# The first product of a gated network in two 64-row tiles of TensorE's array, with copies of its moving operand in the other half

## The chip, the core and the metric

The kernel runs on one core of a Trainium2 chip. Time is device time in microseconds (us) of one execution; the median of three runs before the change is 2152.42 us (2152.29 to 2153.91). PE is TensorE's matmul stream, PEld its weight loads, DVE VectorE, ACT ScalarE, POOL GpSimd and SP SyncE, which issues the transfers.

## What is computed

Four batches of 12480 rows with 128 channels go through attention over 49 agents and then through a two-layer network of width 2048:

```python
def _attn_ref(q, k, v, agents):
    a2k = sm(agents, k)          # softmax(scale * agents @ k.T), 49 x 12480
    agent_v = a2k @ v            # 49 x 128
    q2a = sm(q, agents)          # 12480 x 49
    return q2a @ agent_v
def _moe_ref(x, w_in, w_out):    # 128 -> 2048 -> 128
    h = x @ w_in
    g = h - np.tanh(h)
    return g @ w_out
```

## The kernel before, in words

The kernel folds the attention's last product into the network's first layer. Per batch it computes `agent_v`, multiplies it with `w_in` (`project`), and so has a matrix of 49 x 2048. A row of the output then needs only its 49 softmax weights p: h is p times that matrix. Both are in f32, and a single-pass product keeps fewer bits, so each operand is split in a high and a low part: `awh` and `awl` for the matrix, and for p the two parts stacked. The matrix is held twice, in partitions 0 to 48 and 49 to 97, and the transposed p (`pT`) has its high part in the first 49 partitions and its low part in the next 49. One matmul of 98 rows then gives awh x (p high + p low).

The rows are cut into 100 blocks of up to 500 rows, 25 per batch, and the 2048 hidden columns into 16 chunks of 128; two chunks are a **pair**, so there are 8 pairs per block and 800 in all. For each pair:

- `m1` (L531 to L536): four matmuls of 98 rows and 500 columns on TensorE, for each chunk one with `awh` (L534) and one with `awl` (L535). Their result `h` fills two PSUM banks, one per chunk; there are three such buffers.
- ACT makes `y` = tanh (L544) and `z` = y squared (L546); DVE makes `g` = h times z (L549), a form of h - tanh(h) for small h.
- POOL rounds `g` to its high part `gh` (L578), and DVE takes the low part `gl` (L583).
- `m2` (L596 to L598): six matmuls into the block's accumulator, for each chunk `gh` with the low part of `w_out`, `gh` with its high part, and `gl` with the high part. Every second block's last pair, and the first block, use one f32 matmul per chunk in place of three (L594).

Between the pairs small pieces of other work are started at fixed positions of a pair of blocks: the softmax of the next two blocks (`q_softmax`, L490 to L513), their transposes (`q_transpose`, L521 and the copy to `pT` at L526) at position 13 for the even block and position 2 for the odd one, and the attention over k and v of the next batch (`phase1`, L278, L329 and L339 on TensorE). L278 and L339 use 64 columns of the array, two products at a time in different halves. The order in which an engine gets its instructions is made by a scheduler that plays through the program with estimated times; fixed orders are given only for the first block and, in a few places, for DVE, ACT and POOL. All transfers go through SP's queue in order.

A check at the end (`general`) repeats all with a slower formula where h is too large; it isn't taken with these inputs.

Of the kernel before, what the change touches and what calls it, by code (L numbers as in the profile page):

```python
# [12 lines left out]
F32 = mybir.dt.float32  # L13
F32R = mybir.dt.float32r
# [3 lines left out]
ET = mybir.EngineType  # L18
AF = mybir.ActivationFunctionType
ALU = mybir.AluOpType  # L20
# [3 lines left out]
B, N, C = 4, 12480, 128  # L24
A = 49
A2 = 2 * A
EARLY = 11
HALF = 64
FF = 2048
NCH = FF // 128  # L30
TT = 126
TG = 120
GT = 8
# [4 lines left out]
BT = GT // 2  # L38
BLK = 500
# [57 lines left out]
class Build:  # L97
# [19 lines left out]
    def constants(self):  # L117
        nc = self.nc
        c = self.const
        self.agz = c.tile([128, B, HALF], F32, tag="ag", name="ag")  # L120
        self.ag = self.agz[:, :, :A]
        nc.sync.dma_start(self.ag, self.agT.rearrange("b c a -> c b a"))
        nc.gpsimd.memset(self.agz[:, :, A:], 0.0)
        self.ident = c.tile([128, 128], F32, tag="ident", name="ident")
        make_identity(nc, self.ident)
        self.identr = c.tile([128, 128], F32R, tag="identr", name="identr")
        nc.vector.tensor_copy(self.identr, self.ident)
        self.sel = c.tile([128, A], F32, tag="sel", name="sel")
        for r in (slice(0, HALF), slice(HALF, 128)):
            nc.vector.tensor_copy(self.sel[r], self.ident[r, r.start : r.start + A])  # L130
        self.ones = c.tile([128, 128], F32, tag="ones", name="ones")
        nc.vector.memset(self.ones, 1.0)
        self.mx = c.tile([128, NP * B], F32, tag="mx", name="mx")
        nc.vector.memset(self.mx, 0.0)
        self.w_in = c.tile([128, FF], F32, tag="w_in", name="w_in")
        self.wo_h = c.tile([128, NCH, C], F32R, tag="wo_h", name="wo_h")
        self.wo_l = c.tile([128, NCH, C], F32R, tag="wo_l", name="wo_l")
        self.wo_f = c.tile([128, 2, C], F32, tag="wo_f", name="wo_f")
        self.vb = [c.tile([128, GT, C + 2], F32, tag=f"v{i}", name=f"v{i}") for i in range(VB)]
        self.avs = c.tile([128, B, A2], F32, tag="avs", name="avs")  # L140
        self.aw = {}

    def decode(self, raw, dst, size, rem, ta, tb):
# [51 lines left out]
    def phase1(self, b):  # L195
        nc = self.nc
# [35 lines left out]
        def scores(g):  # L232
# [42 lines left out]
            for c in range(n // 2):  # L275
                for r in range(2):
                    to = ps[HALF * r : HALF * (r + 1), c * 128 : (c + 1) * 128]
                    nc.tensor.matmul(to, self.agz[:, b, :], kt[:, n // 2 * r + c, :], start=True, stop=True)  # L278
# [118 lines left out]
        def sums():  # L397
            yield
            yield
            if b == 0:  # L400
                an, n = st["acc"], HALF + A
                nc.vector.tensor_copy(an[:n, :C], st["ps"][:n, :C])
                pt = self.misc()
                nc.tensor.matmul(pt[:, :A], an[:n, :C], self.sel[:n], start=True, stop=True)
                sm = self.small.tile([128, A], F32, tag="mb", name="mb")
                nc.vector.tensor_scalar(sm, st["pr"], EPS, None, ALU.add)
                nc.vector.reciprocal(sm, sm)
                yield
                two = [128, 2, A]
                nc.vector.tensor_tensor(  # L410
                    self.avs[:, b, :].rearrange("p (two a) -> p two a", a=A),
                    pt[:, None, :A].broadcast_to(two),
                    sm[:, None, :].broadcast_to(two),
                    ALU.mult,
                )
                return
            acc = st["acc"]
            pt = self.misc()
            nc.tensor.matmul(pt[:, :A], acc[:, :C], self.sel, start=True, stop=True)
            rows_of = acc[:, C : C + 1].broadcast_to([128, 128])  # L420
            nc.tensor.matmul(pt[:, A:A2], rows_of, self.sel, start=True, stop=True)
            yield
            sm = self.small.tile([128, A], F32, tag="sm", name="sm")
            nc.vector.tensor_scalar(sm, pt[:, A:A2], EPS, None, ALU.add)
            nc.vector.reciprocal(sm, sm)
            two = [128, 2, A]
            nc.vector.tensor_tensor(
                self.avs[:, b, :].rearrange("p (two a) -> p two a", a=A),
                pt[:, None, :A].broadcast_to(two),
                sm[:, None, :].broadcast_to(two),  # L430
                ALU.mult,
            )

        if b == 0:
            self.mb_at = lambda: st["mb_at"]
# [6 lines left out]
    def project(self, b, bound):  # L442
        nc = self.nc

        def part(c, lo, hi):
            yield
            yield
            if c == 0:
                self.aw[b] = tuple(
                    self.keep.tile([128, FF], F32R, tag=t, name=t, bufs=2) for t in ("awh", "awl")  # L450
                )
            awh, awl = self.aw[b]
            sl = slice(lo, hi)
            if b == 0 and bound and c < 2:
                ps = self.ph.tile([128, 2, 512], F32, tag="h", name="h")[:, 0, :]
            else:
                ps = self.misc()
            ps = ps[:A2, : hi - lo]
            nc.tensor.matmul(ps, self.avs[:, b, :], self.w_in[:, sl], start=True, stop=True)
            yield  # L460
            h = awh[:A2, sl]
            nc.scalar.copy(h, ps)
            nc.vector.tensor_tensor(awl[:A2, sl], ps, h.bitcast(F32), ALU.subtract)
            if bound and b:
                self.bound(b, c, sl)

        cuts = PCUT if b == 0 and bound else (0, 512, 1024, 1536, 2048)
        return [part(c, cuts[c], cuts[c + 1]) for c in range(len(cuts) - 1)]
# [15 lines left out]
    def q_softmax(self, halves, qt, res, TT=TT):  # L484
        nc = self.nc
        ps = self.misc()
        for t in range(GT):
            b, at, w = halves[t // BT]
            at += min(t % BT * TT, w - TT)
            nc.tensor.matmul(ps[:TT, t * A : (t + 1) * A], qt[:, at : at + TT], self.ag[:, b, :], start=True, stop=True)  # L490
            if t % BT == BT - 1:
                yield
        pv = ps[:TT, : GT * A].rearrange("p (t a) -> p t a", a=A)
        m = self.small.tile([128, GT], F32, tag="qm", name="qm")
        e = self.small.tile([128, GT, A], F32, tag="qe", name="qe")
        ev = e[:TT]
        s = self.small.tile([128, GT], F32, tag="qs", name="qs")
        nc.vector.tensor_reduce(m[:TT], pv, axis=AX.X, op=ALU.max)
        nc.scalar.copy(ev, pv)  # L499
        yield  # L500
        nc.gpsimd.tensor_tensor(ev, ev, m[:TT, :, None].broadcast_to([TT, GT, A]), ALU.subtract)  # L501
        yield
        nc.scalar.activation(ev, ev, AF.Exp, scale=SCALE)
        yield
        nc.vector.tensor_reduce(s[:TT], ev, axis=AX.X, op=ALU.add)
        nc.vector.tensor_scalar(s[:TT], s[:TT], EPS, None, ALU.add)
        nc.vector.reciprocal(s[:TT], s[:TT])
        nc.vector.tensor_tensor(ev, ev, s[:TT, :, None].broadcast_to([TT, GT, A]), ALU.mult)
        yield
        pp = self.small.tile([128, GT, A2], F32R, tag="pp", name="pp")  # L510
        nc.scalar.copy(pp[:TT, :, :A], ev)  # L511
        yield
        nc.gpsimd.tensor_tensor(pp[:TT, :, A:], ev, pp[:TT, :, :A].bitcast(F32), ALU.subtract)  # L513
        res.append(pp)

    def q_transpose(self, pp, half, res, w, TT=TT):
        nc = self.nc
        ps = self.misc()
        for t in range(BT):
            at = min(t * TT, w - TT)  # L520
            nc.tensor.transpose(  # L521
                ps[:A2, at : at + TT].bitcast(F32R), pp[:TT, half * BT + t, :], self.identr[:TT, :TT]
            )
        yield
        pT = self.keep.tile([128, BLK], F32R, tag="pT", name="pT", bufs=3)
        nc.scalar.copy(pT[:A2, :w], ps[:A2, :w])  # L526
        res.append(pT)

    def m1(self, aw, pT, i, w):
        nc = self.nc  # L530
        h = self.ph.tile([128, 2, 512], F32, tag="h", name="h")  # L531
        for c in range(2):
            sl = slice((2 * i + c) * 128, (2 * i + c + 1) * 128)
            nc.tensor.matmul(h[:, c, :w], aw[0][:A2, sl], pT[:A2, :w], start=True, stop=False)  # L534
            nc.tensor.matmul(h[:, c, :w], aw[1][:A2, sl], pT[:A2, :w], start=False, stop=True)  # L535
        return h[:, :, :w]  # L536

    def pair(self, t):
# [364 lines left out]
```

## Time and profile before

| | |
|---|---|
| median of three runs | 2152.42 us (2152.29 to 2153.91) |
| span of the profiled execution | 2150.6 us |
| the profiled execution's own time beside the span | not recorded; the runs' median is 1.8 us longer |
| busy: PE, PEld | 2126.8, 1713.6 us |
| busy: DVE, ACT, POOL | 1998.3, 1828.1, 1313.8 us |
| granted clock of TensorE, mean | 0.998 |
| transfers | 108.69 MB, 15.1% of 16 engines' span |

A row of a group gives line, engine, operation, output <- inputs, the shape and count, then busy time and mean duration in ns, then the idle time of the engine just before, and what ended it. In rows of the timeline the first number is the start in us from the span's start and the second the time to the end of the row's last instruction; a row with x16 holds sixteen in a row. Matmuls are pipelined, so a duration is longer than the distance to the next start. An f32 matmul leaves two records. `98*128` is the number of rows and columns of the array that are in use.

### The profile page before, as it was taken

The page shows a single profiled execution, that of the slowest core. Times are in us where ns is not written, and L with a number is a line of the kernel's source. Part 1 is how long each engine was busy: PE and PEld are TensorE (multiplying, and loading weights), DVE is VectorE, ACT ScalarE, POOL GpSimd, SP SyncE. Part 2 cuts the span into 40 slices and gives each one's busy share as a digit, 9 for nine tenths or more (in the row PEclk, how much of TensorE's full clock was granted, in tenths as well). Part 3 has the DMA queues.
Part 4 walks back from the last instruction along what each step waited for, and adds up shares of the span by engine and source line. Part 5 has one row for each costly group of instructions (what it writes and reads, how often), then busy time and mean ns, then how long its engine had stood idle before and what let it go on. Part 6 is the DMA issues. An engine that isn't in the chain of part 4 may idle for free.

```text
span 2150.6 us, 30293 instructions
## 1 busy us (share of the span) xinstructions
PE 2126.8 (99%) x10859; PEld 1713.6 (80%) x10859; DVE 1998.3 (93%) x2031; ACT 1828.1 (85%) x2136; POOL 1313.8 (61%) x858
## 2 busy tenths in 40 slices
PE   8999999999999999999999999999999999999998
PEld 7587878877877887888787778878878888888886
DVE  7999998889999998889999999988999999999998
ACT  3888888888888888888898888888889889899896
POOL 0365566556665565556675557655566767777666
PEclk9999999999999999999999999999999999999999
DMA  9321112110111111111002110111000000000000
GB/s 350 96 67 60 52 34 73 51 49 29 39 49 59 60 50 49 59 61 49 20 20 68 59 42 28 51 59 41 28 31 20 29 30 20 29 29 20 29 10 21
DMA packets 65325, 108.69 MB, mean 51 GB/s; under 512 B 3984, under 2 KB 44176, under 8 KB 65168
## 3 DMA queue, kind: packets, MB, share of 16 engines
q1 hardware_dynamic: 65168, 106.68, 15.1%
q8 instruction: 89, 1.46, 0.3%
q14 instruction: 68, 0.56, 0.1%
HBM read 81.10 MB, written 25.56 MB: 50 GB/s over the span
## 4 chain that ended last, share of the span: by engine, by line
PE 95%; DVE 2%; POOL 1%; issue 1%; ACT 0%; DMA 0%; POOLq 0%; SPq 0%; DVEq 0%
PE h L534 17%; PE h L535 16%; PE misc L598 16%; PE misc L596 15%; PE misc L597 15%; PE misc L594 4%; PE misc L490 4%; PE misc L339 2%; PE misc L278 2%; PE misc L521 1%; PE h L249 1%; POOL gh L578 1%; DVE g L549 1%; PE misc L329 1%; DVE gl L583 1%
## 5 line engine op out<-in xcount | busy, mean ns | idle before, releaser
L578 POOL TENSOR_SCALAR gh<-g 128x1000 fp32r<-128x1000 f32 (+1 forms) x743 | 1172.7, 1579 | 702.9 <-DVE g L549 357.9
L583 DVE TENSOR_TENSOR gl<-g,gh 128x1000 fp32r<-128x1000 f32 (+1 forms) x743 | 952.8, 1284 | 99.9 <-PE misc L598 58.9
L549 DVE TENSOR_TENSOR g<-h,z 128x1000 f32<-128x1000 f32 (+1 forms) x800 | 946.1, 1187 | 24.6 <-ACT z L546 20.6
L544 ACT ACTIVATE y<-h 128x1000 f32<-128x1000 f32 (+1 forms) x800 | 799.0, 1002 | 191.6 <-PE h L535 187.6
L546 ACT ACTIVATE z<-y 128x1000 f32<-128x1000 f32 (+1 forms) x800 | 828.8, 1040 | 21.2 <-DVE g L549 4.2
L534 PE MATMUL h<-pT,awh 98*128 98x500 f32 (+1 forms) x1600 | 662.1, 414 | 0.1
L535 PE MATMUL h<-pT,awl 98*128 98x500 f32 (+1 forms) x1600 | 623.1, 389 | 0.0
L598 PE MATMUL misc<-gl,wo_h 128*128 128x500 f32 (+1 forms) x1486 | 589.5, 397 | 3.7 <-DVE gl L583 3.7
L596 PE MATMUL misc<-gh,wo_l 128*128 128x500 f32 (+1 forms) x1486 | 579.0, 390 | 2.8 <-POOL gh L578 2.8
L597 PE MATMUL misc<-gh,wo_h 128*128 128x500 f32 (+1 forms) x1486 | 578.1, 389 | 0.0
L534 PEld LDWEIGHTS h<-pT,awh 98*128 98x128 f32 x1600 | 301.2, 188 | 77.4 <-issue 14.0
L535 PEld LDWEIGHTS h<-pT,awl 98*128 98x128 f32 x1600 | 303.0, 189 | 67.7 <-issue 14.7
L598 PEld LDWEIGHTS misc<-gl,wo_h 128*128 128x128 f32 x1486 | 279.1, 188 | 70.0 <-DVE gl L583 10.5
L596 PEld LDWEIGHTS misc<-gh,wo_l 128*128 128x128 f32 x1486 | 280.8, 189 | 62.6 <-POOL gh L578 7.8
L597 PEld LDWEIGHTS misc<-gh,wo_h 128*128 128x128 f32 x1486 | 279.7, 188 | 54.5
L501 POOL TENSOR_TENSOR qe<-qe,qm 126x392 f32<-126x392 f32 x50 | 69.7, 1395 | 65.3 <-ACT qe L499 65.3
L513 POOL TENSOR_TENSOR pp<-qe,pp 126x392 fp32r<-126x392 f32 x50 | 67.8, 1357 | 58.4 <-ACT pp L511 56.6
L490 PEld LDWEIGHTS misc<-ag,qt 128*126 128x126 f32 x800 | 95.9, 190 | 3.9
L490 PE MATMUL misc<-ag,qt 128*126 128x49 f32 x800 | 93.4, 269 | 0.0
L594 PE MATMUL misc<-g,wo_f 128*128 128x500 f32 (+1 forms) x196 | 89.9, 581 | 0.0
L754 ACT ACTIVATE o<-misc 128x500 f32<-128x500 f32 (+1 forms) x100 | 58.2, 582 | 21.7 <-PE misc L598 11.7
L526 ACT CAST pT<-misc 98x500 fp32r<-98x500 f32 (+1 forms) x100 | 56.7, 568 | 7.4 <-PE misc L521 6.5
(111 smaller groups left out, 840.5 us busy)
## 6 DMA issues: line engine op xcount, KB each, us to landing
kt<-kT SPq DMA_DIRECT2D x48, 512.0 KB, 3.7
qt<-qT SPq DMA_DIRECT2D x46, 500.0 KB, 3.4
outT<-o SPq DMA_DIRECT2D x46, 500.0 KB, 2.6
v<-v SPq DMA_DIRECT2D x36, 512.0 KB, 4.1
vt<-v SPq DMA_DIRECT2D x12, 512.0 KB, 7.1
raw<-w_in SPq DMA_DIRECT2D x4, 512.0 KB, 9.0
v<-w_out SPq DMA_DIRECT2D x4, 512.0 KB, 8.9
qt<-qT SPq DMA_DIRECT2D x4, 490.0 KB, 3.4
```

Of the source, the lines that this page charges most:

```text
L490: nc.tensor.matmul(ps[:TT, t * A : (t + 1) * A], qt[:, at : at + TT], self.ag[:, b, :], start=True, stop=True)
L534: nc.tensor.matmul(h[:, c, :w], aw[0][:A2, sl], pT[:A2, :w], start=True, stop=False)
L535: nc.tensor.matmul(h[:, c, :w], aw[1][:A2, sl], pT[:A2, :w], start=False, stop=True)
L544: nc.scalar.activation(self.pair(y), h, AF.Tanh, scale=TSC)
L546: nc.scalar.activation(z, y, AF.Square)
L549: nc.vector.tensor_tensor(self.pair(g), h, self.pair(z), ALU.mult)
L578: self.nc.gpsimd.tensor_scalar(gh, g, 1.0, 0.0, ALU.mult, ALU.add)
L583: self.nc.vector.tensor_tensor(gl, g, gh.bitcast(F32), ALU.subtract)
L594: nc.tensor.matmul(acc[:, :w], wf[:, c * C : (c + 1) * C], gh[:, x], start=first, stop=last)
L596: nc.tensor.matmul(acc[:, :w], self.wo_l[:, f, :], gh[:, x], start=first, stop=False)
L597: nc.tensor.matmul(acc[:, :w], self.wo_h[:, f, :], gh[:, x], start=False, stop=False)
L598: nc.tensor.matmul(acc[:, :w], self.wo_h[:, f, :], gl[:, x], start=False, stop=last)
```

## The change

The two parts of p are no longer multiplied in one matmul of 98 rows. The high part now stands in partitions 0 to 48 and the low part in 64 to 112 (`HALF` is 64, `PW` is 113), the matrices `awh` and `awl` are held in both places (`av2`), and two transfers per block copy the parts of p to the other half into a second tile, `pb`. In `m1` the first chunk of a pair uses only partitions 0 to 48, the second only 64 to 112: each is a product of 49 rows in its own 64-row half of the array. A chunk needs three terms: awh x p low, awl x p high and awh x p high. The term awl x p low is left out. The matmuls are written alternately for the two chunks, and their order among themselves is fixed. `pT` has two buffers instead of three, and `pb` has two. The tiles for the softmax's result (`pp`) are two fixed ones, cleared once.

```diff
@@ q_softmax
-        pp = self.small.tile([128, GT, A2], F32R, tag="pp", name="pp")
+        pp = self.ppb[self.npp % 2]
+        self.npp += 1
         nc.scalar.copy(pp[:TT, :, :A], ev)
         yield
-        nc.gpsimd.tensor_tensor(pp[:TT, :, A:], ev, pp[:TT, :, :A].bitcast(F32), ALU.subtract)
+        nc.gpsimd.tensor_tensor(pp[:TT, :, HALF:PW], ev, pp[:TT, :, :A].bitcast(F32), ALU.subtract)
@@ project
             if c == 0:
+                for at in (0, HALF):
+                    nc.vector.tensor_copy(self.av2[:, at : at + A], self.avs[:, b, :])
...
-            nc.tensor.matmul(ps, self.avs[:, b, :], self.w_in[:, sl], start=True, stop=True)
+            nc.tensor.matmul(ps, self.av2, self.w_in[:, sl], start=True, stop=True)
@@ q_transpose
-        pT = self.keep.tile([128, BLK], F32R, tag="pT", name="pT", bufs=3)
-        nc.scalar.copy(pT[:A2, :w], ps[:A2, :w])
-        res.append(pT)
+        pT = self.keep.tile([128, BLK], F32R, tag="pT", name="pT", bufs=2)
+        nc.scalar.copy(pT[:PW, :w], ps[:PW, :w])
+        pb = self.keep.tile([128, BLK], F32R, tag="pb", name="pb", bufs=2)
+        nc.sync.dma_start(pb[HALF:PW, :w].bitcast(F32), pT[:A, :w].bitcast(F32))
+        nc.sync.dma_start(pb[:A, :w].bitcast(F32), pT[HALF:PW, :w].bitcast(F32))
+        res.append((pT, pb))
@@ m1
-        for c in range(2):
-            sl = slice((2 * i + c) * 128, (2 * i + c + 1) * 128)
-            nc.tensor.matmul(h[:, c, :w], aw[0][:A2, sl], pT[:A2, :w], start=True, stop=False)
-            nc.tensor.matmul(h[:, c, :w], aw[1][:A2, sl], pT[:A2, :w], start=False, stop=True)
+        high, low = pT, pT[::-1]
+        first = self.count()
+        for n, (weights, p) in enumerate(((aw[0], low), (aw[1], high), (aw[0], high))):
+            for c, r in enumerate((slice(0, A), slice(HALF, PW))):
+                sl = slice((2 * i + c) * 128, (2 * i + c + 1) * 128)
+                nc.tensor.matmul(h[:, c, :w], weights[r, sl], p[c][r, :w], start=n == 0, stop=n == 2)
+        self.issue_order(ET.PE, first)
```

How the scheduler places the new instructions, the following pieces of the order show. First TensorE before the change, in the middle of the program: the first product of a pair (L534, L535) and then the second product of an earlier one.

```order
L534 MATMUL h<-pT,awh 128x500
L535 MATMUL h<-pT,awl 128x500
L534 MATMUL h<-pT,awh 128x500
L535 MATMUL h<-pT,awl 128x500
L598 MATMUL misc<-gl,wo_h 128x500
L596 MATMUL misc<-gh,wo_l 128x500
L597 MATMUL misc<-gh,wo_h 128x500
L598 MATMUL misc<-gl,wo_h 128x500
L596 MATMUL misc<-gh,wo_l 128x500
L597 MATMUL misc<-gh,wo_h 128x500
```

Ten matmuls all use the whole height of the array. The same place of TensorE's order after the change (the first product is L539 there, the second L601 to L603):

```order
L539 MATMUL h<-pb,awh 128x500
L539 MATMUL h<-pT,awh 128x500
L539 MATMUL h<-pT,awl 128x500
L539 MATMUL h<-pb,awl 128x500
L539 MATMUL h<-pT,awh 128x500
L539 MATMUL h<-pb,awh 128x500
L603 MATMUL misc<-gl,wo_h 128x500
L601 MATMUL misc<-gh,wo_l 128x500
L602 MATMUL misc<-gh,wo_h 128x500
L603 MATMUL misc<-gl,wo_h 128x500
L601 MATMUL misc<-gh,wo_l 128x500
L602 MATMUL misc<-gh,wo_h 128x500
```

Six matmuls of half the array's height now stand between those of the full height; the first reads `pb`, the tile that the transfers fill. The third place is the start of an even block on TensorE after the change (numbers tell the tiles apart: h_6818 and h_6843 are two pairs' results, pb_6776 and pT_6774 the new block's p).

```order
L601 MATMUL misc_6673<-gh_6785,wo_l_89 128x500
L602 MATMUL misc_6673<-gh_6785,wo_h_88 128x500
L539 MATMUL h_6818<-pb_6776,awh_5298 128x500
L539 MATMUL h_6818<-pT_6774,awh_5298 128x500
L539 MATMUL h_6818<-pT_6774,awl_5299 128x500
L539 MATMUL h_6818<-pb_6776,awl_5299 128x500
L539 MATMUL h_6818<-pT_6774,awh_5298 128x500
L539 MATMUL h_6818<-pb_6776,awh_5298 128x500
L539 MATMUL h_6843<-pb_6776,awh_5298 128x500
L539 MATMUL h_6843<-pT_6774,awh_5298 128x500
L539 MATMUL h_6843<-pT_6774,awl_5299 128x500
L539 MATMUL h_6843<-pb_6776,awl_5299 128x500
```

The block's first pairs moved to behind the second products of the block before, 18 of which stand between this block's transposes (L520) and the first row that reads pb_6776; three pairs' first products, 18 matmuls, then follow each other.

More of the change, by code (lines that the diff above doesn't have):

```diff
@@ L28 @@
 HALF = 64
+PW = HALF + A
 FF = 2048
@@ L130, in constants @@
             nc.vector.tensor_copy(self.sel[r], self.ident[r, r.start : r.start + A])
-        self.ones = c.tile([128, 128], F32, tag="ones", name="ones")
-        nc.vector.memset(self.ones, 1.0)
+        self.one = c.tile([128, 1], F32, tag="ones", name="ones")
+        nc.vector.memset(self.one, 1.0)
+        self.ones = self.one.broadcast_to([128, 128])
         self.mx = c.tile([128, NP * B], F32, tag="mx", name="mx")
@@ L139, in constants @@
         self.vb = [c.tile([128, GT, C + 2], F32, tag=f"v{i}", name=f"v{i}") for i in range(VB)]
-        self.avs = c.tile([128, B, A2], F32, tag="avs", name="avs")
+        self.avs = c.tile([128, B, A], F32, tag="avs", name="avs")
+        self.av2 = c.tile([128, PW], F32, tag="av2", name="av2")
+        nc.gpsimd.memset(self.av2, 0.0)
+        self.ppb = [c.tile([128, GT, PW], F32R, tag=f"pp{i}", name=f"pp{i}") for i in range(2)]
+        for t in self.ppb:
+            nc.gpsimd.memset(t.bitcast(F32), 0.0)
+        self.npp = 0
         self.aw = {}
@@ L408, in sums @@
                 yield
[L409 to L415, printed above, removed]
+                nc.vector.tensor_tensor(self.avs[:, b, :], pt[:, :A], sm, ALU.mult)
                 return
@@ L425, in sums @@
             nc.vector.reciprocal(sm, sm)
[L426 to L432, printed above, removed]
+            nc.vector.tensor_tensor(self.avs[:, b, :], pt[:, :A], sm, ALU.mult)
         if b == 0:
@@ L457, in part @@
                 ps = self.misc()
-            ps = ps[:A2, : hi - lo]
-            nc.tensor.matmul(ps, self.avs[:, b, :], self.w_in[:, sl], start=True, stop=True)
+            ps = ps[:PW, : hi - lo]
+            nc.tensor.matmul(ps, self.av2, self.w_in[:, sl], start=True, stop=True)
             yield
-            h = awh[:A2, sl]
-            nc.scalar.copy(h, ps)
-            nc.vector.tensor_tensor(awl[:A2, sl], ps, h.bitcast(F32), ALU.subtract)
+            h = awh[:PW, sl]
+            nc.scalar.copy(h, ps[:PW])
+            nc.vector.tensor_tensor(awl[:PW, sl], ps[:PW], h.bitcast(F32), ALU.subtract)
             if bound and b:
@@ L521, in q_transpose @@
             nc.tensor.transpose(
-                ps[:A2, at : at + TT].bitcast(F32R), pp[:TT, half * BT + t, :], self.identr[:TT, :TT]
+                ps[:PW, at : at + TT].bitcast(F32R), pp[:TT, half * BT + t, :PW], self.identr[:TT, :TT]
             )
         yield
-        pT = self.keep.tile([128, BLK], F32R, tag="pT", name="pT", bufs=3)
-        nc.scalar.copy(pT[:A2, :w], ps[:A2, :w])
-        res.append(pT)
+        pT = self.keep.tile([128, BLK], F32R, tag="pT", name="pT", bufs=2)
[4 more added lines that the diff above has]
+        res.append((pT, pb))
     def m1(self, aw, pT, i, w):
```

## The prediction

> **What bounds the kernel now.** I read the share of each engine first, then the chain of work that ended last, then the costliest groups.
>
> ```profile
> PE 2126.8 (99%) x10859; PEld 1713.6 (80%) x10859; DVE 1998.3 (93%) x2031; ACT 1828.1 (85%) x2136; POOL 1313.8 (61%) x858
> PE 95%; DVE 2%; POOL 1%; issue 1%; ACT 0%; DMA 0%; POOLq 0%; SPq 0%; DVEq 0%
> L534 PE MATMUL h<-pT,awh 98*128 98x500 f32 (+1 forms) x1600 | 662.1, 414 | 0.1
> L535 PE MATMUL h<-pT,awl 98*128 98x500 f32 (+1 forms) x1600 | 623.1, 389 | 0.0
> ```
>
> TensorE is busy 99% of the span and is 95% of the chain, and the two lines of the first product are 3200 of its records, four for each of the 800 pairs. A busy PE is not a PE at its peak, so the price of one matmul is read as the distance from its start to the next start, in the timeline of TensorE in the middle of the span (start, duration, what):
>
> ```profile
> 1003.02 0.39 PE L534 MATMUL h<-pT,awh 98*128 98x500 f32 x1
> 1003.25 0.40 PE L535 MATMUL h<-pT,awl 98*128 98x500 f32 x1
> 1003.48 0.39 PE L534 MATMUL h<-pT,awh 98*128 98x500 f32 x1
> 1003.71 0.39 PE L535 MATMUL h<-pT,awl 98*128 98x500 f32 x1
> 1003.94 0.39 PE L598 MATMUL misc<-gl,wo_h 128*128 128x500 f32 x1
> ...
> 1005.31 0.39 PE L598 MATMUL misc<-gl,wo_h 128*128 128x500 f32 x1
> ```
>
> Ten starts from 1003.02 to 1005.31 are 0.229 us apart on average; over longer undisturbed stretches I get 0.227, and use that. A pair is four such steps of the first product and six of the second, 2.27 us, with no gap for a weight load: the load of the next matrix runs under the matmul before. So whatever shortens or lengthens TensorE's stream moves the end one for one, until DVE (1998 us busy) binds.
>
> **The removed matmul.** Six matmuls per pair replace four, but two at a time. If two tiles run together, a pair of chunks takes three steps instead of four: 800 x 0.227 = **-182 us**. The trace has no pair of row tiles. Nearest is a pair of column tiles, L278, where two 64-column products share the array:
>
> ```profile
> 84.34 0.39 PE L596 MATMUL misc<-gh,wo_l 128*128 128x500 f32 x1
> 84.57 0.38 PE L597 MATMUL misc<-gh,wo_h 128*128 128x500 f32 x1
> 84.88 1.09 PE L278 MATMUL misc<-kt,ag 128*64 128x128 f32 x16
> 85.91 0.49 PE L534 MATMUL h<-pT,awh 98*128 98x500 f32 x1
> 86.23 0.38 PE L535 MATMUL h<-pT,awl 98*128 98x500 f32 x1
> 86.46 0.39 PE L534 MATMUL h<-pT,awh 98*128 98x500 f32 x1
> 302.94 0.60 PE L329 MATMUL misc<-ident,s 128*128 128x128 f32 x4
> ```
>
> L329 moves 128 f32 columns through the whole array in 0.109 us a record (four records in 0.60, the last 0.27 long). The 16 records of L278, of the same 128 columns, stand in 1.03 us, 0.064 each, changes of shape included: two run at once. I take the same for row tiles. Bounds: -182 if they do, +363 (two steps more, 2 x 0.227 x 800) if they don't.
>
> **The price of a change of shape.** The same rows show it. From the start of L597 (84.57) to L278 is 0.31 where 0.227 is usual, so +0.085. Eight double steps of 0.109 would bring the next start to 85.75, and it is 85.91: +0.16, of which 0.05 is L278's first load (64 columns), and 0.10 the way back. The first full matmul then takes 0.32 to the next instead of 0.227, +0.10, since its load could not run ahead. Altogether 86.23 - 84.57 = 1.66 us, where 0.227 + 0.87 + 0.227 = 1.32 would do: 0.34 for the way in and out. That this holds for rows too, one place shows, where a product of 128 rows is followed by one of 64 on the same line and then by a full one:
>
> ```profile
> 49.78 0.39 PE L380 MATMUL h<-s,ones 128*128 128x49 f32 x2
> 50.09 0.18 PEld L380 LDWEIGHTS h<-s,ones 64*128 64x128 f32 x1
> 50.10 0.31 PE L380 MATMUL h<-s,ones 64*128 64x49 f32 x1
> 50.24 0.27 PE L380 MATMUL h<-s,ones 64*128 64x49 f32 x1
> 50.44 0.18 PEld L490 LDWEIGHTS misc<-ag,qt 128*126 128x126 f32 x1
> 50.45 0.31 PE L490 MATMUL misc<-ag,qt 128*126 128x49 f32 x1
> ```
>
> The second of the first row's two starts at 49.89 (0.39 less one duration of 0.28). To the 64-row product are 0.21 us and from the second of these back to 128 rows again 0.21, where this line's steps are 0.11: +0.09 each way, with no wait named, and the load starts only when the matmul does. The Trainium skill, TensorEngine Tiling (Array Packing), section Key Properties, says that changing the tiling mode drains TensorE; it gives no price, these rows do.
>
> A row tile loads 128 columns, not 64, so its first load costs 0.10 like the one on the way back: 2 x (0.09 + 0.10) = 0.39 us in and out, 0.195 a change. Below, 0.17 (L278 as it stands); above, 0.25, if the two tiles' first loads come one after the other.
>
> How often: in the order of TensorE's instructions the first product now stands in 713 separate stretches, 569 of them just one pair (the first two places quoted above). All changes of shape together are 1536, and 168 before (84 stretches of column tiles): 1368 more. 1368 x 0.195 = **+267 us** (233 to 342).
>
> **Split pairs.** In 64 stretches the count is odd (5, 7, 11), since a pair is cut by second-product matmuls; there one tile runs alone for half a step's worth: 64 x 0.5 x 0.227 = **+7 us**.
>
> **Bursts.** In the third place quoted above several pairs' first products stand in a row; 74 stretches hold ten or more, where before 39 held eight or more. TensorE hands out a pair in 0.68 us there, and three buffers of h then wait for the other engines:
>
> ```profile
> L549 DVE TENSOR_TENSOR g<-h,z 128x1000 f32<-128x1000 f32 (+1 forms) x800 | 946.1, 1187 | 24.6 <-ACT z L546 20.6
> L583 DVE TENSOR_TENSOR gl<-g,gh 128x1000 fp32r<-128x1000 f32 (+1 forms) x743 | 952.8, 1284 | 99.9 <-PE misc L598 58.9
> ```
>
> DVE gives a buffer back every 1.19 + 1.28 = 2.47 us. Between nothing and one g (1.19) per burst is late, 0 to 85 us; I take half a microsecond for 70: **+35 us**.
>
> **Already paid.** L534 has a mean of 414 ns and L535 389 though their shapes agree: now and then the first load of a pair waits and isn't hidden even today. 25 ns x 1600 = 40 us at most fall together with a change of shape; much of it is after the f32 products of L594, so **-10 us**.
>
> **The copies of p.** Two transfers per block and the wait for them are new. In time the transposed p is ready when ACT has copied it, and the rows for a like transfer are the last three:
>
> ```profile
> 1008.49 0.41 PE L521 MATMUL misc<-identr,pp 126*98 126x126 f32 x4
> 1010.20 0.57 ACT L526 CAST pT<-misc 98x500 fp32r<-98x500 f32 x1
> 1014.35 0.34 SPq L481 DMA_DIRECT2D qt<-qT  x1
> ag<-agT SPq DMA_DIRECT2D x1, 98.0 KB, 2.3
> kt<-kT SPq DMA_DIRECT2D x4, 128.0 KB, 2.1
> ```
>
> From the transposes to pT are 2.3 us here; two issues of 0.34 on SP and 2.3 us until 98 KB have landed make 5.3. The first matmul of a block reads the second copy. Behind the transposes of an odd block TensorE has over 8 us of other work; in the even ones the order puts 12 to 20 matmuls, some 3.3 to 6 us, so the copy is late by a little in about 24. Behind a waiting first product stands all of TensorE's queue. I take 24 x 0.4 = **+10 us**; above, 50 blocks x 2 us = 100 (SP is in order, and a store or a k load that waits stands ahead of some copies); below, nothing. The other edits (113 rows for 98 in the transposes, projection and copies, two small copies on DVE per batch, clears on POOL at the start) change no column count of a matmul and lie under TensorE's stream.
>
> **The sum.** -182 + 267 + 7 + 35 - 10 + 10 = +127 us. The profiled span is 2150.6 us and the median of the runs 2152.4, so 1.8 us lie outside: 2150.6 + 127 + 1.8 = **2280 us**, 5.9% slower.
>
> **Rivals.** *Cheap changes, faster (10%).* If the next shape's weights were loaded ahead as between ordinary matmuls, a change would cost 0.09 and 1368 of them 123: 2152 - 182 + 123 + 7 + 35 - 10 + 10 = 2135 us. The sign turns at (182 - 7 - 35 + 10 - 10) / 1368 = 0.102 us a change. For it speaks that a weight load is normally hidden; against it that the loads of L380 and L490 start with their matmuls. *First loads one after the other (10%):* 713 x 0.107 (L329's pace for 128 columns) = 76, 2356 us. *Copies late (6%):* 100 instead of 10, 2370 us. *Loads not under the own tile's matmul (5%):* two of three steps pay 0.10 more, 1600 x 0.103 = 165, 2445 us; L278's steps of 0.109 speak against it. That is what the Trainium skill, TensorE: Matmul & The Clock Gate, section The mechanism, says of tiles: a load overlaps matmuls in flight only if the row group differs. No run here shows row tiles. *Tiles don't run together (7%):* the change would not do what it says; 2152 + 363 + 267 + 35 - 10 + 10 = 2817 us.
>
> **How the numbers follow.** The forecast keeps 62%. Its own bounds (price 0.17, no burst stalls, 40 us already paid) reach down to 2152 + 127 - 34 - 35 - 30 = 2180 and up, with the first two dear rivals, to about 2375; I give **2190 to 2375**, which leaves out the cheap changes, the loads and the separate tiles. A measurement tells 0.2%, 4 us. Faster 10%, the first rival; the same 3%, from between it and the forecast; slower 87%.
>
> **What would show it.** In the profile after: L539's records in twos a few ns apart, three steps of 0.227 in a stretch; 0.31 to 0.33 us into and out of each; PE still near 99%, DVE's share falling to some 88%. A stretch of six records that takes 1.4 us in all instead of 1.1 would mean serial loads; a row "PE h L539 <- DMA pb" with more than 30 us, late copies. If the way in and out of a stretch costs under 0.2 us, the prediction is wrong in its largest term.

## The result, and the profile after

The changed kernel takes 2341.54 us (median of three, 2339.74 to 2345.2) against 2152.42: a ratio of 1.0878, 95% interval 1.0859 to 1.0898. It is **189 us slower**; the forecast was 127 us slower, 2280 us. The profiled execution has a span of 2338.0 us at a granted clock of 0.994.

The page of the changed kernel (busy time of each engine, shares of the chain that ended last, two of the costliest groups):

```profile
PE 2257.2 (97%) x12459; PEld 1487.1 (64%) x12459; DVE 2001.1 (86%) x2039; ACT 1820.3 (78%) x2136; POOL 1288.7 (55%) x861
PE 59%; DVE 14%; ACT 9%; POOL 9%; issue 6%; DMA 2%; SPq 0%; POOLq 0%; DVEq 0%; ACTq 0%
L539 PE MATMUL h<-pb,awh 49*128 49x500 f32 (+1 forms) x1600 | 666.5, 436 | 17.0 <-DVE g L554 12.9
L603 PE MATMUL misc<-gl,wo_h 128*128 128x500 f32 (+1 forms) x1486 | 642.2, 432 | 29.0 <-DVE gl L588 27.2
```

TensorE's busy time rose by 2257.2 - 2126.8 = 130 us and its idle time by (2338.0 - 2257.2) - (2150.6 - 2126.8) = 57 us. These are two losses. The first stands in an undisturbed stretch of TensorE's timeline (start, duration, what):

```profile
1008.17 0.39 PE L602 MATMUL misc<-gh,wo_h 128*128 128x500 f32 x1
1008.40 0.38 PE L603 MATMUL misc<-gl,wo_h 128*128 128x500 f32 x1
1008.71 0.49 PE L539 MATMUL h<-pb,awh 49*128 49x500 f32 x1
1008.71 0.49 PE L539 MATMUL h<-pT,awh 49*128 49x500 f32 x1
1009.05 0.38 PE L539 MATMUL h<-pT,awl 49*128 49x500 f32 x1
1009.05 0.39 PE L539 MATMUL h<-pb,awl 49*128 49x500 f32 x1
1009.27 0.39 PE L539 MATMUL h<-pT,awh 49*128 49x500 f32 x1
1009.28 0.39 PE L539 MATMUL h<-pb,awh 49*128 49x500 f32 x1
1009.60 0.49 PE L601 MATMUL misc<-gh,wo_l 128*128 128x500 f32 x1
1009.92 0.39 PE L602 MATMUL misc<-gh,wo_h 128*128 128x500 f32 x1
```

The two tiles of a step start within 10 ns of each other here, so the array does run them together. But where an ordinary step is 0.227, the way in is 0.31, the first step 0.34, the second 0.22, the way out 0.33 and the next full matmul's step 0.32. Over the 572 stretches of just six records the medians, each taken from the first tile of a step, are 0.313, 0.333, 0.226, 0.322 and 0.330: four dear steps, 0.086 + 0.106 + 0.095 + 0.103 = 0.39 us for going in and out, to save one step of 0.227.

The second loss, 6 us earlier in the same timeline (in brackets the idle time before the row, and who ended it):

```profile
999.94 0.39 PE L539 MATMUL h<-pb,awh 49*128 49x500 f32 x1
999.95 0.39 PE L539 MATMUL h<-pT,awh 49*128 49x500 f32 x1
1001.09 0.49 PE L539 MATMUL h<-pb,awh 49*128 49x500 f32 x1 [0.76 <-DVE g L554]
...
1002.27 0.50 PE L601 MATMUL misc<-gh,wo_l 128*128 128x500 f32 x1 [0.24 <-POOL gh L583]
```

and the waits of TensorE by what ended them (us in total, times, longest):

```profile
PE misc L603 <- DVE gl L588: 27.2, 62, 0.9
PE misc L601 <- POOL gh L583: 14.9, 48, 0.9
PE h L539 <- DVE g L554: 12.9, 15, 2.0
...
PE h L539 <- DMA pb<-pT: 3.5, 8, 0.8
```

Several pairs' first products stand in a row here; TensorE has handed out all buffers of h and waits for DVE's g, and then the second products wait for gh and gl. By these rows the transfers of p cost 3.5 us. That turned out to be the wrong way to read them (third group of experiments).

### The profile page after: what moved, and what is told of

It is laid out like the page before. It is cut to its first block, busy times and chain, and to the rows that moved or that the text cites. A ratio compares the mean times of both kernels' runs of the same rounds, so it can differ in the third digit from the quotient of the medians.

```text
span 2338.0 us, 33908 instructions
## 1 busy us (share of the span) xinstructions
PE 2257.2 (97%) x12459; PEld 1487.1 (64%) x12459; DVE 2001.1 (86%) x2039; ACT 1820.3 (78%) x2136; POOL 1288.7 (55%) x861
## 4 chain that ended last, share of the span: by engine, by line
PE 59%; DVE 14%; ACT 9%; POOL 9%; issue 6%; DMA 2%; SPq 0%; POOLq 0%; DVEq 0%; ACTq 0%
PE h L539 18%; PE misc L603 12%; PE misc L601 10%; PE misc L602 9%; DVE g L554 7%; POOL gh L583 7%; DVE gl L588 6%; ACT z L551 4%; ACT y L549 3%; PE misc L488 3%; PE misc L599 2%; POOL qe L499 1%; DMA pb<-pT 1%; PE misc L286 1%; PE misc L347 1%
## 5 line engine op out<-in xcount | busy, mean ns | idle before, releaser
L583 POOL TENSOR_SCALAR gh<-g 128x1000 fp32r<-128x1000 f32 (+1 forms) x743 | 1137.6, 1531 | 813.1 <-DVE g L554 650.5
L539 PE MATMUL h<-pb,awh 49*128 49x500 f32 (+1 forms) x1600 | 666.5, 436 | 17.0 <-DVE g L554 12.9
L539 PE MATMUL h<-pT,awh 49*128 49x500 f32 (+1 forms) x1600 | 670.5, 431 | 0.0
L603 PE MATMUL misc<-gl,wo_h 128*128 128x500 f32 (+1 forms) x1486 | 642.2, 432 | 29.0 <-DVE gl L588 27.2
L601 PE MATMUL misc<-gh,wo_l 128*128 128x500 f32 (+1 forms) x1486 | 604.4, 407 | 16.6 <-POOL gh L583 14.9
L539 PEld LDWEIGHTS h<-pb,awh 49*128 49x128 f32 x1600 | 289.8, 184 | 275.3 <-issue 116.3
L603 PEld LDWEIGHTS misc<-gl,wo_h 128*128 128x128 f32 x1486 | 279.5, 188 | 244.8 <-issue 96.4
L601 PEld LDWEIGHTS misc<-gh,wo_l 128*128 128x128 f32 x1486 | 281.0, 189 | 128.3 <-issue 50.5
L539 PE MATMUL h<-pb,awl 49*128 49x500 f32 (+1 forms) x800 | 312.1, 390 | 0.0
L539 PEld LDWEIGHTS h<-pT,awh 49*128 49x128 f32 x1600 | 295.3, 185 | 24.6 <-issue 0.7
L539 PE MATMUL h<-pT,awl 49*128 49x500 f32 (+1 forms) x800 | 310.5, 388 | 0.0
L539 PEld LDWEIGHTS h<-pT,awl 49*128 49x128 f32 x800 | 149.4, 187 | 10.1 <-issue 8.0
L539 PEld LDWEIGHTS h<-pb,awl 49*128 49x128 f32 x800 | 149.4, 187 | 2.1 <-issue 0.4
```

What stands on the lines that cost most here:

```text
L539: nc.tensor.matmul(h[:, c, :w], weights[r, sl], p[c][r, :w], start=n == 0, stop=n == 2)
L583: self.nc.gpsimd.tensor_scalar(gh, g, 1.0, 0.0, ALU.mult, ALU.add)
L601: nc.tensor.matmul(acc[:, :w], self.wo_l[:, f, :], gh[:, x], start=first, stop=False)
L603: nc.tensor.matmul(acc[:, :w], self.wo_h[:, f, :], gl[:, x], start=False, stop=last)
```

## The experiments

### What one change of shape costs

The kernel before, with one small matmul ahead of each pair's first product, into columns of h that are overwritten: once over the full 98 rows, once over 49 (a 64-row tile). The two kernels differ in nothing else.

```diff
+        first = self.count()
+        nc.tensor.matmul(h[:, 0, :64], aw[0][:A2, :128], pT[:A2, :64], start=True, stop=True)   # d_full
+        nc.tensor.matmul(h[:, 0, :64], aw[0][:A, :128], pT[:A, :64], start=True, stop=True)     # d_rows
...
+        self.issue_order(ET.PE, first)
```

> The kernel before, with one small extra matmul (98 rows, 128 columns of the array, 64 columns moved) ahead of each pair's first product, into the same PSUM bank, which the next matmul overwrites; it keeps the array's full height. It is the control of the run with 64-row tiles. Theory (a change of shape has a price of its own, about 0.2 us, that a full-height matmul does not pay): the extra matmul only uncovers one weight load, 0.11 us, since a matmul of 64 columns is too short to hide the next load: 800 x 0.11 = 88, 2240 us (2215 to 2265). Rival (any extra short matmul with its load costs the 0.4 us of an excursion): about 2470 us.

> The kernel before, with the same small extra matmul, of 49 rows instead of 98: it uses a 64-row tile, so the array changes its shape twice per pair and nothing else differs; the order of TensorE's instructions is the control's. Theory (0.195 to 0.20 us a change, two loads uncovered): 0.31 us from the matmul before, 0.22 to 0.25 to the next, 0.33 to the second next, against 3 x 0.227 less the extra one: 0.40 to 0.43 a pair, 800 x 0.41 = 330, 2480 us (2455 to 2510), some 240 above the control. Rival (the loss in the changed kernel comes from waits of its order and from its copies, not from the shape): like the control, 2240 us.

Measured: 2255.33 us (1.0467, 1.0449 to 1.0484) and 2472.53 us (1.1472, 1.1453 to 1.1492). The difference of the two is 217.2 / 800 = 0.27 us a pair for the shape alone; against the kernel before, the 64-row excursion costs 318.3 / 800 = 0.40 us. TensorE's timeline of the full-height kernel, then of the other:

```profile
1001.91 0.39 PE L537 MATMUL h<-pT,awl 98*128 98x500 f32 x1
1002.14 0.20 PE L533 MATMUL h<-pT,awh 98*128 98x64 f32 x1
1002.17 0.47 PE L536 MATMUL h<-pT,awh 98*128 98x500 f32 x1
1002.48 0.39 PE L537 MATMUL h<-pT,awl 98*128 98x500 f32 x1
```

```profile
1001.94 0.39 PE L601 MATMUL misc<-gl,wo_h 128*128 128x500 f32 x1
1002.26 0.29 PE L533 MATMUL h<-pT,awh 49*128 49x64 f32 x1
1002.48 0.50 PE L536 MATMUL h<-pT,awh 98*128 98x500 f32 x1
1002.81 0.39 PE L537 MATMUL h<-pT,awl 98*128 98x500 f32 x1
```

At full height the small matmul is entered at the usual 0.23 and left after 0.03, its own 64 columns; the next step is 0.31, since 0.03 us cannot hide the load behind it. With 49 rows the way in is 0.32, the way out 0.22 and the next step 0.33. Less the 0.03 of its own work and the two ordinary steps, 0.32 + 0.22 + 0.33 - 0.03 - 0.454 = 0.39: the same price as in the changed kernel, and 0.195 a change, as forecast. The edit holds no copies and no clears, and TensorE's order is the control's, record for record. So 0.27 us is shown to belong to the row count alone. The other 0.12 the control pays too, since its matmul is too short to hide a load; that the changed kernel, whose matmuls are long, pays the whole 0.39 its own rows show.

### Do the two tiles run together, and are their loads hidden?

The changed kernel with both chunks of a pair in partitions 0 to 48, so that the six matmuls must share one half of the array.

```diff
-            for c, r in enumerate((slice(0, A), slice(HALF, PW))):
+            for c, r in enumerate((slice(0, A), slice(0, A))):
```

> The changed kernel with both chunks of a pair in the lower half of the array, partitions 0 to 48 (the second chunk reads the weights of that half and the other part of p, so its terms are not those of the reference). Order and number of the matmuls stay; only the running of two at a time goes. Theory (two row tiles run at the same time, so a pair takes three steps): six steps, 3 x 0.222 x 800 = 533 more, 2875 us (2840 to 2900), steps of 0.222. Rival (half of the array is no faster or slower alone, the pairs gain less than they seem): less than 300 more, 2640 us.

Measured 2936.0 us (two runs, 2914.71 and 2957.29; ratio 1.3628, 1.3514 to 1.3742), 594 us over the changed kernel and above the 2840 to 2900 that were expected. Its timeline of TensorE:

```profile
1500.63 0.49 PE L539 MATMUL h<-pb,awh 49*128 49x500 f32 x1
1500.96 0.38 PE L539 MATMUL h<-pT,awh 49*128 49x500 f32 x1
1501.18 0.39 PE L539 MATMUL h<-pT,awl 49*128 49x500 f32 x1
1501.41 0.38 PE L539 MATMUL h<-pb,awl 49*128 49x500 f32 x1
...
1503.06 0.62 PE L601 MATMUL misc<-gh,wo_l 128*128 128x500 f32 x1
1503.48 0.62 PE L602 MATMUL misc<-gh,wo_h 128*128 128x500 f32 x1
```

Six steps one after another now. Over its 572 stretches of six records the medians are 0.333 for the first step and 0.225 to 0.229 for the others, and a stretch takes 1.557 us up to the next full matmul where the changed kernel's takes 0.880: in different halves the tiles overlap fully, in one half not at all. That is 0.677 x 800 = 542 of the 594 us. These steps also settle the rival on loads: all six use the same rows of the array, and every step after the first still costs 0.225 to 0.229, with a load of its own weights in it. By the Trainium skill, TensorE: Matmul & The Clock Gate, section The mechanism, a load overlaps matmuls in flight only if the row group (the rows of the array that are used) differs. The measurement decides: the loads are hidden. The last two rows, at 0.42 a step, are a surprise; see the last section.

### Where the other 60 us come from

The changed kernel with both halves reading pT and no transfers (the first chunk then leaves out the low part of p, the second the high part); and the same with the transfers issued but read by nobody.

```diff
-        pb = self.keep.tile([128, BLK], F32R, tag="pb", name="pb", bufs=2)       # no_copies
-        nc.sync.dma_start(pb[HALF:PW, :w].bitcast(F32), pT[:A, :w].bitcast(F32))
-        nc.sync.dma_start(pb[:A, :w].bitcast(F32), pT[HALF:PW, :w].bitcast(F32))
-        res.append((pT, pb))                                                     # both kernels
+        res.append((pT, pT))
```

> The changed kernel without the two transfers per block: each half of the array reads its part from pT itself in all three terms, so the first chunk gets no low part and the second no high part of p; the matmuls, their shapes and their count stay. Theory (the copies are hidden but for 3.5 us of named waits; the loss above the forecast is waiting of TensorE on DVE and POOL that the many pipeline breaks cause): 2330 us (2318 to 2340). Rival (the copies, and the order that the scheduler makes around them, hold the 60 us by which the forecast was too low): 2280 us.

> The changed kernel with both transfers per block left in, but with no reader: the matmuls read pT alone, as in the run without copies, and TensorE's order is that run's to the last row. Theory (the 62 us lie in the order and the waits that the first products' dependence on the copies brings, not in the transfers): like the run without copies, 2280 us (2274 to 2290). Rival (the transfers themselves cost it: SP's queue, the write into pT's neighbour, the memory's ports): like the changed kernel, 2335 us.

Measured 2279.37 us (1.0578, 1.056 to 1.0595) and 2281.20 us (1.0584, 1.0566 to 1.0601). The first is where the rival put it, not the theory; the second is where the theory put it. So the 20 MB of transfers and their issues on SP cost nothing that can be told from zero (2 us, inside both intervals); that the first products *depend* on them costs 62. Where it went, the waits of the kernel without copies show:

```profile
PE misc L600 <- DVE gl L585: 10.8, 23, 0.6
...
PE misc L598 <- POOL gh L580: 5.1, 21, 0.9
```

Hardly any first product waits for g any more, gl fell from 27.2 to 10.8 and gh from 14.9 to 5.1. TensorE's idle time is 34 us (span 2278.1, busy 2243.8), against 81; another 13 us are less busy time.

If lateness is the cause, an earlier start must give the 62 us back with the copies in place. In the changed kernel, the pair ahead of which the even block's p is transposed was moved three pairs forward:

```diff
-T0 = 13
+T0 = 10
```

> The changed kernel with one number changed: the transposes for the next even block start at position 10 of 16 instead of 13, three pairs (about 8 us) earlier, so that the copies have landed before the block begins. The stretches of 18 matmuls at the block starts are gone from the order. Theory (the copies come too late for the even blocks, which delays their first products, in the order and on the chip): 2285 us (2275 to 2300), TensorE idle near 30 us. Rival (the wait for the copies is not what costs): 2335 to 2345 us.

Measured **2269.57 us** (1.0535, 1.0517 to 1.0552), 72 us below the changed kernel, 10 below the one without copies and below the range of the theory. TensorE's idle time is 32 us. The waits:

```profile
PE misc L601 <- POOL gh L583: 6.5, 28, 0.4
...
PE misc L603 <- DVE gl L588: 3.9, 7, 1.1
...
PE h L539 <- DMA pb<-pT: 0.8, 1, 0.8
```

So it was the dependence on the copies after all, though hardly a row named it. TensorE's instructions are put in line by what is expected to be ready. In the changed kernel 32 records (median of the even blocks) stand between a block's transposes and its first product, which starts 5.9 us after them; without copies it is 16 records and 3.8 us. The copies' last packet ends 4.5 us after the transposes (median), and TensorE's rows show a wait for it in only eight places: what is late is mostly the place in the order. Meanwhile ACT gets no h, first with the copies, then without (waits of ACT: us in total, times, longest):

```profile
ACT y L549 <- PE h L539: 226.0, 268, 4.8
```

```profile
ACT y L546 <- PE h L536: 125.6, 242, 3.9
```

That is 0.84 us a wait with the copies and 0.52 without (0.53 in the kernel before, in 353 waits). What ACT gets late DVE and POOL get late, and TensorE then waits for them: from the third block on, 35 us of the changed kernel's idle time stand within 40 records of a block's start, and 2 us without copies. The trace books that wait on DVE and POOL, the last to finish, not on the transfer that had shifted the order. This chain is read from the rows; no run changes the order alone. The rows of three pairs are not enough to explain it: there are 18 stretches of 18 records in the changed kernel and none with T0 = 10, but also 12 in the kernel without copies, and TensorE doesn't wait in those or in the 24 records behind them. There the first product before such a stretch is 5.5 us back, in the changed kernel 8.1 us (medians).

What part of the 62 us is the order and what part the transfer itself these runs do not separate; an earlier transpose changes both. Nor does any run have T0 = 10 without copies, so part of the 72 us may come from the transposes' new place alone.

This is the best form of the change that was run, and still 5% behind the kernel before.

### Can the price be shared by more work?

If one way in and out costs 0.39 and a pair saves 0.227, two pairs to a stretch would save 0.45 and come out ahead. TensorE was made to follow the order in which the program is written: second products three pairs behind the first (`LAG2`), T0 = 10, first products of one pair, or of two, together. The kernel before in the same kind of order, with its T0 left at 13, is the control.

```diff
-LAG2 = 1
+LAG2 = 3
...
+        self.issue_order(ET.PE, early)
...
-            h = self.m1(self.aw[blocks[n][0]], pT[n][0], i, width(n))            # double_ordered alone
+            for j in {0: (0, 1), 2: (2, 3), 4: (4, 5), 6: (6, 7)}.get(i, ()):
+                ahead[j] = self.m1(self.aw[blocks[n][0]], pT[n][0], j, width(n))
+            h = ahead.pop(i)
```

> The changed kernel with the transposes of the even block at position 10 (copies in time) and TensorE held in the program's order, with the second product three pairs behind the first in it, so that DVE and POOL have time; each pair's first product stands alone: 795 stretches. Theory (0.2 us a change, 1508 more than in the kernel before; nothing else): 302 - 182 + 5 on top of the kernel before, 2280 us, with 0 to 30 us of waits: 2295 (2275 to 2320). Rival (the loss is of the scheduler's order, not of the changes): below 2230 us.

> The same kernel, but the first products of two pairs stand together, so that there are 399 stretches instead of 795: 767 changes fewer, the work is the same. Theory (0.2 us a change): 153 us less than the run with single pairs, 2140 us, plus waits for the three buffers of h, up to 60: 2165 us (2135 to 2215). It can at best tie with the kernel before. Rival (the price belongs to each row-tiled matmul, not to the change of shape): the same time as the run with single pairs.

> The control of both: the kernel before with TensorE held in the program's order, the second product three pairs behind the first. Theory (the order costs nothing where TensorE is fed): 2155 us (2145 to 2175). Rival (such an order makes TensorE wait): 2250 us or more, and then the two runs above hold that loss too.

Measured: single pairs 2288.34 us (1.0621, 1.0603 to 1.0639), two pairs 2281.34 (1.0594, 1.0576 to 1.0612), before in order 2221.10 (1.0314, 1.0297 to 1.0331). The first is as expected; the other two are not. Halving the stretches, 798 to 400, saved 7 us where 398 x 0.39 = 155 was due. That is the rival's time, but not its reason: inside a stretch of twelve the steps behind the first are 0.225 to 0.227 (medians), and the ways in and out are 0.313 and 0.325, with single pairs 0.313 and 0.323. So the price still belongs to the change of shape. The page's busy times and first wait of the two-pair kernel:

```profile
PE 2162.9 (95%) x12459; PEld 1513.2 (66%) x12459; DVE 2147.6 (94%) x2039; ACT 1821.2 (80%) x2136; POOL 1236.9 (54%) x861
```

```profile
PE misc L603 <- DVE gl L588: 61.4, 116, 1.3
```

TensorE's busy time fell from 2243.2 in the single-pair kernel to 2162.9, by 80; its idle time rose by 71. A stretch of twelve takes 1.56 us at the median but 1.68 on average, since in some the second pair waits for a buffer of h. DVE, 2061.4 us busy in the single-pair kernel, is now at 94% of the span and named in the largest wait. About half of the missing 148 us shows as this idle time; the rest I could not place. Written order with the second product three pairs behind costs the kernel before 67 us, so none of these three says what the change would be worth under a better order.

Two more kernels failed to answer what they were built for. In one, TensorE followed the written order of the changed kernel as it stood, to test the bursts:

```diff
+        self.issue_order(ET.PE, early)
```

> The changed kernel with TensorE's instructions held in the order in which the program is written, so that each pair's first product stands alone in the order and no bursts are left: 795 stretches instead of 713, 137 more changes of shape. Theory (bursts at the block starts make TensorE wait for DVE and POOL, some 50 us): +27 for the changes, -45 for the waits, 2324 us (2300 to 2340), with TensorE idle below 45 us. Rival (the waits don't come from bursts): +27 alone, 2368 us, with TensorE idle near 80 us.

It took 2791.77 us (1.2962, 1.2941 to 1.2984), which neither theory had, with one row of waits that covers half of it:

```profile
PE misc L603 <- DVE gl L588: 243.9, 347, 2.4
```

In that order the second product follows one pair behind the first, and gl is late 347 times. It says nothing of bursts (first products of several pairs in a row). In the other the second product is cut into 64-row tiles too, so that hardly any change of shape is left between them; its two halves are summed on POOL:

```diff
-            nc.tensor.matmul(acc[:, :w], self.wo_l[:, f, :], gh[:, x], start=first, stop=False)
...
+            terms = (self.wo_l, gh), (self.wo_h, gh), (self.wo_h, gl)
+            for k, (wo, m) in enumerate(terms):
+                for a, r in zip(acc, halves):
+                    nc.tensor.matmul(a[:, :w], wo[r, f, :], m[r, x], start=first and k == 0, stop=last and k == 2)
```

> A version meant to keep the saved step without the changes of shape: the second product too is cut into two 64-row tiles, each with its own accumulator in PSUM, added on POOL at the block's end (h has two buffers instead of three to make room). TensorE's instructions are held in the program's order with the second product one pair later than written before, and the transposes of the even block start at position 11. Changes of shape are left only around the small pieces, some 670, 500 more than in the kernel before. Theory (a change costs 0.2 us, two tiles run at once in the second product as in the first): -182 + 100 and 0.005 us less for each of 4458 steps, -22: 2050 us if nothing else waits; with two buffers of h DVE and ACT may be late, 2050 to 2200. Rival (tiles in the second product don't run at once, since both read the same weights' columns and accumulate): 4458 steps more, over 3000 us.

It took 2500.68 us (1.1607, 1.1588 to 1.1627), above the 2050 to 2200 of the theory and below the rival's 3000. As a test of the mechanism it is clear (timeline of TensorE; x2 is two tiles at once):

```profile
1003.77 0.39 PE L607 MATMUL misc<-gh,wo_l 64*128 64x500 f32 x2
...
1004.90 0.39 PE L607 MATMUL misc<-gl,wo_h 64*128 64x500 f32 x2
1005.12 0.38 PE L539 MATMUL h<-pT,awh 49*128 49x500 f32 x1
...
1005.80 0.39 PE L607 MATMUL misc<-gh,wo_l 64*128 64x500 f32 x2
```

From 1003.77 to 1005.80 a pair takes nine steps of 0.226, 2.03 us, where the kernel before takes 2.27 and the changed one 2.27 - 0.227 + 0.39 = 2.43. Between one 64-row product and another of 64 rows there is no price, though 49 rows follow 64. It does not become time. The two extra accumulators leave room for only two buffers of h, and the wait for them is the largest of TensorE's 291 us of idle time (span 2498.6, busy 2208.0):

```profile
PE h L539 <- DVE g L554: 150.5, 174, 2.6
```

TensorE's busy time is 81 us above the kernel before too, at a granted clock of 0.963 and in a written order. What each of these costs no run separates.

## Why the prediction was right, and where it was too small

The side and the cause were right; 62 of the 189 us were not seen.

- **The removed matmul (-182).** Shown. Two tiles start within 10 ns; forced into one half they take 0.225 to 0.229 each, one after another, and the kernel 594 us more, 542 of them in these steps.
- **The price of a change of shape (+267 at 0.195).** Shown twice: 0.39 us in and out in the changed kernel's own rows, and 0.39 with the added 64-row matmul, 0.27 of it against a control that differs in the row count alone. The first step has a median of 0.333 with two tiles' loads in it and of 0.333 with one (both chunks in one half), so the loads do not come one after the other; the later steps of 0.225 to 0.229 hide them. Both rivals on loads fall, and cheap changes (under 0.102) too.
- **Split pairs (+7) and already paid (-10)** are too small for these runs to tell apart; nothing was tried on them.
- **The sum without copies.** -182 + 267 + 7 + 35 - 10 = +117 was forecast; the kernel without copies measured 2279.37 - 2154.2 = +125. That these two, and the forecast of 2280 with them, lie so close is partly luck, since errors of both signs stand inside. *Bursts (+35)* hardly show there: TensorE's idle time is 34 us against 24 before. The order without copies has 1416 changes of shape more than the kernel before, for the 1368 counted, which at 0.195 is another 9 us. And *the transposes*, put at nothing among "the other edits" since they change no column count, cost 13 us of TensorE's busy time. Some 11 us stay unplaced. The transposes load 113 columns for 98; no run changes that alone. Their group grew from

```profile
L521 PE MATMUL misc<-identr,pp 126*98 126x126 f32 x400 | 41.7, 227 | 0.8 <-POOL pp L513 0.8
```

  in the kernel before to, without copies (busy us, mean ns of one; the changed kernel has 55.3 and 260),

```profile
L520 PE MATMUL misc<-identr,pp 126*113 126x126 f32 x400 | 55.0, 260 | 0.5 <-POOL pp L512 0.5
```

- **The copies of p (+10).** This is the term that failed. Its size measured 2341.5 - 2279.4 = 62. The step reasoned that a copy which is late by 0.4 us in 24 blocks costs 24 x 0.4. The time of the copies was about right (landed 4.5 us after the transposes, for 5.3), and TensorE waits for them by name for only 3.5 us. The upper bound of 100 and the rival of late copies (2370 us) lie above the truth, and their reason, transfers that are held up in SP's queue, is not what the runs show: the transfers alone cost 2 us. What the step left out is what an operand that is expected late does to the order: first products slide back, ACT, DVE and POOL get their work later, and TensorE then waits for DVE and POOL. The sign to look for was also wrong: "PE h L539 <- DMA pb with more than 30 us" reads 3.5, while the dependence costs 62.
- **The shares.** DVE's fell to 86%, where 88% was given: the span grew more than forecast, and the work of DVE did not (2001.1 us for 1998.3). TensorE's fell to 97%, where 99% was given: that is the idle time of the 62 us.

## What to carry to other kernels

Price a change of array shape before cutting a product into tiles: here 0.39 us for a way in and out, which one step of 0.227 saved cannot pay. At least two must be saved per stretch, or the neighbours cut into the same shape, and the engines that feed and empty the stretch must keep up with it. When a new operand depends on a transfer, find out what its dependence costs by reading something else in its place: the wait may be booked on engines that are not the cause. And an engine at 93% behind one at 99% is the next bound: with two pairs to a stretch TensorE's busy time fell by 80 us and its idle time rose by 71, most of it waiting for DVE.

## What was not expected of the hardware

In the kernel with both chunks in one half the granted clock fell while TensorE was busy all the time. Two rows of its windows (from:to, us, PE busy and records, PEld, DVE, ACT, POOL, granted clock, DMA share, GB/s):

```profile
500.00:1000.00 500.00, 497.38 (x2084) 344.82 (x2083) 346.97 (x335) 309.52 (x355) 198.38 (x142) 0.91 0.13 41
...
2500.00:2950.00 450.00, 448.20 (x1820) 306.82 (x1819) 349.88 (x307) 302.15 (x330) 215.06 (x145) 1.00 0.07 24
```

It shows as full matmuls that start 0.42 apart for a while, as quoted above (the granted clock is 0.50 from 1502 to 1505 us), and it makes up part of the 594 us. TensorE hardly waits in either window (497 of 500 and 448 of 450 us busy), so idling does not explain it. Long runs of matmuls in one half of the array alone are what this kernel has and the others lack. But two other kernels that do wait, the written order (0.958) and the all-tile one (0.963), show dips too, and no run separates these causes.
